# Centred sums of squares on ScalarE in the norm statistics, without VectorE's variance steps and two shift columns

## The chip, the core and the metric

One core of one Trainium2 chip runs one fused transformer block. The metric is the device time of one execution in microseconds. Before the change the median of three runs is 200.81 us (200.79 to 201.29).

The engines are named as in the profile: PE (TensorE matmuls), PEld (its weight loads), DVE (VectorE), ACT (ScalarE), POOL (GpSimd) and SP (SyncE, which issues DMAs). Each engine works through its own queue in order.

## What is computed

The reference, cut to its core (S = 2048 rows, D = 512, 32 heads of 16, F = 1792, all bf16):

```python
def _layernorm(x, eps=1e-05):
    m = mean(x); v = var(x)
    return (x - m) / sqrt(v + eps)

sa, ca, ga, sb, cb, gb = (silu(c) @ w_mod) split in six
h = _layernorm(x) * (1 + ca) + sa
x = x + ga * A(h)          # qkv; attention over 8 keys, 2 apart, looking back; output projection
h = _layernorm(x) * (1 + cb) + sb
x = x + gb * B(h)          # B: layernorm again, then an MLP over the rows (2048 -> 1792 -> 2048)
```

So each row tile passes three layernorms: of the input (called 1 in the names), of the sum after attention (2), and inside B (3).

## The kernel before

The 2048 rows are 16 tiles of 128 rows, one row per partition. They are worked in five chunks of 2, 4, 4, 4 and 2 tiles (SIZES). For each chunk: norm 1, a transposition, q, k and v (names qkv, their copies out of PSUM ev), products of q and shifted k on DVE (qk), their sums over a head on PE (red), softmax (max, sub, exp, esum, rcp, smB), products of the weights with shifted v on DVE (pv), their sums on PE (pvacc), the output projection (wo) with the residual (x1), norm 2 with its scale and shift (aff), and norm 3. The MLP's first matmul sums over all 2048 rows, so its parts (mlp1) start as soon as tiles leave norm 3; mlp2 and the output follow.

**What sets the order.** Every piece of work is put into a graph as a named operation with the engines that could run it (lines 43 to 84). The string ORDER (lines 192 to 251) lists all names in the order in which they are issued; a letter behind the colon picks the engine (`ln3s1:a` on ACT, `n1_2:d` on DVE, `n2_1:p` on POOL). `schedule` (line 86) walks the string, hands out PSUM and SBUF slots, and each engine's queue is the string filtered by engine. "fill" entries are matmuls without use, which keep PE at work. All instructions are recorded by one helper at line 143, so the profile has L143 for nearly every line, and groups are told apart by tile names.

**The norms.** The names that matter are these; the number at the end is the row tile, or the first tile of the group.

- `ln1s`, `ln2s`, `ln3s` (`ln_stats`, line 387): the statistics of one tile. On DVE one bn_stats. On ACT two passes over the tile: an Identity scaled by 1/D whose accumulator gives the mean (tile mv, column 0), and a Square scaled by D to the power -0.5 whose accumulator gives the mean of squares (tile st6).
- `ln1v`, `ln3v` (line 405): a small DVE operation. After bn_stats it is bn_aggr; after the ACT passes it computes mean of squares minus square of the mean into mv, column 1.
- `x1` and `ln2q` (lines 862 to 878): for norm 2 of tiles 0 to 13. The copy of the projection out of PSUM accumulates the row sum (tile sums, column 0), and a Square pass on ACT (`ln2q`) accumulates D times the sum of squares (column 1).
- `ln2m` (lines 887 to 896): two small DVE operations for each group of tiles, the square of the sum and its difference from column 1.
- `rstd` (`ln_rstd`, line 407): two small ACT operations, Ln of the variance plus eps, and Exp of -0.5 times that.
- `nb` (line 418): a small DVE operation, minus mean times rstd.
- `n1`, `n2`, `h3` (`ln_norm`, line 422): the normalised tile, x times rstd plus nb, on ACT, DVE or POOL.

In the profile the tiles of these are mv, st, lv, rs, nb, sums, junk (the unused full-size output of the ACT passes), xx (the rows), and h (h2, h3 and their rings).

The places that the prediction uses stand like this in ORDER:

- Around `max1` (the softmax of chunk 1, with statistics of chunk 3 among it): `... ln1s14:a ... ln1v14 nb1_3 ... mrows1 ... ln1v15 vd0_1 max1 sub1:q ...`
- Around the copy of the last columns of k for chunk 3 (`halo_k3`, on ACT, which overwrites a part of k and so waits for DVE's `qk2_2`): `x1_1:a ln2q1:a x1_0:a xt10 ln2q0:a qk2_1 ... qk2_2 a2_1_0:s halo_k3:a ln2m0 vd1_2 ... pv1_2 rstd1_4 ... nb1_4 ... rstd2_0`
- Around `max3`: `... ln2m2 pv2_0 pvacc2_0 vd3_0 ev4_20:a ln3s0:a ln3v0 ev4_12:a rstd2_2 ev4_22:a ln3v1 ... ln2m4 rstd2_4 nb2_2 n2_2:a max3 sub3:q`
- Around `qk4_1`: `... pv3_3 red4_0 ln2m6 ... qk4_1 ... rstd2_6 ... nb2_6 ... qk4_2 ... qk4_3`

Of the kernel before, what the change touches and what calls it, by code (L numbers as in the profile page):

```python
# [198 lines left out]
qvb_cp0:a ev0_00:a ln1s12:a ev0_02:d qkv1_13 ld_wqkv2 qkv0_20 ln1v13 qk0_3 qk0_2 ev1_13:a qk0_0 qvb1 ln1v12 qkv0_22:q
ld_wrow0 red0_0 ev1_00:a qkv1_03:q ev1_10:a qk0_1 red0_1 red0_2 red0_3 mask qvb_cp1:a ev0_20:a ev0_22:a wsc1_2:p  # L200
halo_v1:a qk1_0 ev1_03:a wsc1_3:a qkv1_11:q ld_wmod2 wsc2_3:a modrow0 ld_b1 mrows0:a ev1_11:a ld_wrow2 qkv1_02:q max0
wsc0_2:p ld_wo0 n1_7:p sub0:q rstd1_3 qkv1_01:q ld_wo2 exp0 qkv1_12:q wsc1_1:p esum0:q qk1_3 red1_0 ev1_01:a qk1_1
ev1_02:a biascols:q n1_6:p ld_wrow1 rcp0 smB0 ev1_12:a ld_x_4_14 ln1s14:a qkv1_22:q qk1_2 a2_0_2:a xt6 ld_wrow3 modrow1
red1_1 a2_0_1:a n1_9:p wsc2_0:d ln1s15:a ln1v14 nb1_3 n1_11:a qkv1_23:q mrows1 qkv1_21:q ev1_21:a red1_2 red1_3 xt8
ev1_23:a fill:1:q n1_10:p qkv1_20:q ev1_20:a ev1_22:a qkv2_13:q qkv2_10:q wsc0_1:p vd0_2 ev2_13:a ln1v15 vd0_1 max1
sub1:q qkv2_00:q exp1 a2_0_0:s a2_0_3:s pv0_1 vd0_0 pv0_0 st_row0 pv0_2 qkv2_03:q esum1:q ld_wo3 pvacc0_0 vd0_3
halo_v2:p biascols_cp:a pvacc0_1 pv0_3 pvacc0_2 pvacc0_3 ev2_10:a ev2_00:a qk2_0 n1_13:a n1_12:a ld_row0 woq_s rcp1
smB1 oev0_2:a qkv2_11:q qkv2_02:q ev2_03:a qk2_3 qkv2_01:q red2_0 oev0_0:a wo0:q wsc2_1:a wsc2_2:a qkv2_12:q ev2_11:a
ev2_01:a ev2_02:a ev2_12:a wo1:q qkv2_21:q a2_1_1:a qkv2_22:q x1_1:a ln2q1:a x1_0:a xt10 ln2q0:a qk2_1 qkv2_23:q xt12
qk2_2 a2_1_0:s halo_k3:a ln2m0 vd1_2 a2_1_2:s qkv3_12:q a2_1_3:s pv1_2 rstd1_4 red2_1 nb1_4 vd1_0 st_row1 red2_2 red2_3  # L210
rstd2_0 ev2_22:a nb2_0 ev2_21:a qkv3_13:q ev3_13:a max2 vd1_3 pv1_0 n1_14:a vd1_1 pvacc1_2 n1_15:a qkv2_20:q ev2_20:a
sub2:q qkv3_22:q ev3_12:a pv1_1 qkv3_10:q exp2 ev2_23:a halo_v3:a qkv3_20:q n2_0:a oev1_2:a ev3_10:a esum2:q rcp2
qkv3_00:q ev3_22:a qkv3_02:q ev3_00:a pv1_3 ev3_02:a pvacc1_0 ev3_20:a qkv3_01:q ev3_01:a qkv3_11:q xt14 ld_row1 n2_1:p
vd2_3 pvacc1_1 smB2 aff0 qk3_0 vd2_1 fill:1:q vd2_0 oev1_0:a oev1_1:a pvacc1_3 ev3_11:a qk3_1 qkv3_23:q oev1_3:a
a2_2_2:s ln3s1:a qkv3_03:q wo4:q a2_2_1:s qk3_2 a2_2_0:s ev3_03:a ev3_23:a x1_4:a ln2q4:a wo2:q x1_2:a a2_2_3:s red3_0
wo3:q x1_3:a ln2q3:a qkv3_21:q ev3_21:a wo5:q red3_1 pv2_3 x1_5:a vd2_2 qk3_3 qkv4_20:q red3_2 qkv4_22:q red3_3
qkv4_12:q fill:18:q ln2q5:a ld_w1_0_512 ln2q2:a ln2m2 pv2_0 pvacc2_0 vd3_0 ev4_20:a ln3s0:a ln3v0 ev4_12:a rstd2_2
ev4_22:a ln3v1 qkv4_02:q oev2_0:a ln2m4 rstd2_4 nb2_2 n2_2:a max3 sub3:q exp3 pvacc2_3 oev2_3:a qkv4_10:q pv2_2 vd3_2
esum3:q nb2_4 pv2_1 vd3_1 n2_3:p ld_w1_0_0 n2_5:a rcp3 smB3 pvacc2_2 fill:14:q a2_3_0:s a2_3_1:s a2_3_3:s n2_4:a
qkv4_00:q oev2_2:a rstd3_0 aff2 pvacc2_1 oev2_1:a wo6:q wo9:q wo7:q aff4 nb3_0 ln3s2:d ev4_02:a ln3s3:a ln3v3 h3_1:p  # L220
wo8:q a2_3_2:s ev4_00:a ln3v2 ld_w2_0 ln3s4:d rstd3_2 nb3_2 x1_9:a ln3s5:a h3_0:p mlp1_0_6_0:q x1_7:a ln3v4 x1_8:a
h3_3:d mlp1_0_1_0:q h3_2:d mlp1_0_6_2:q mlp1_0_1_2:q pv3_1 mlp1_0_5_0:q ln3v5 ev4_10:a ld_w1_0_896 x1_6:a mlp1_0_3_0:q
mlp1_0_3_2:q ln2q7:a pvacc3_1 rstd3_4 mlp1_0_5_2:q oev3_1:a mlp1_0_2_0:q pv3_0 mlp1_0_2_2:q nb3_4 h3_4:a mlp1_0_0_0:q
mlp1_0_0_2:q h3_5:a mlp1_0_0_4:q qk4_0 ln2q8:a ln2q6:a park0_0:a ln2q9:a mlp1_0_6_4:q mlp1_0_2_4:q mlp1_0_1_4:q
park0_1:a pv3_2 mlp1_0_5_4:q vd3_3 pvacc3_0 oev3_0:a mlp1_0_3_4:q ld_w2_1 park0_2:a pv3_3 red4_0 ln2m6 pvacc3_2
oev3_2:a mlp1_0_4_0:q qk4_1 pvacc3_3 ld_w1_0_1152 mlp1_0_4_2:q mlp1_0_4_4:q rstd2_6 oev3_3:a wo12:q halo_v4:p vd4_2
vd4_3 nb2_6 n2_9:a qk4_2 n2_7:d qk4_3 wo10:qn red4_1 ld_w1_0_1408 n2_6:a vd4_1 n2_8:a aff6 red4_2 red4_3 max4 park0_3:a
ln3s8:d ln3s6:d x1_12:a ln3v8 wo11 vd4_0 ln3s9:d mlp1_0_7_0 ld_w2_3 park0_4:a ln3v6 mlp1_0_7_2 park0_5:a ln3v9 x1_11:a
ln2q12:a mlp1_0_8_0 mlp1_0_8_2 park0_6:a wo13:n ln3s7:a ln3v7 sub4 mlp1_0_10_0 mlp1_0_9_0 x1_13:d exp4 rstd3_6 nb3_6
esum4 mlp1_0_8_4 ln2q13:a ln2m12 mlp1_0_10_2 mlp1_0_10_4 mlp1_0_9_2 rcp4 mlp1_0_7_4 h3_8:d rstd2_12 mlp1_0_12_0  # L230
mlp1_0_12_2 mlp1_0_12_4 smB4 a2_4_1:a a2_4_0:s mlp1_0_9_4 a2_4_2:s h3_9:d a2_4_3:a h3_7:d nb2_12 h3_6:p mlp1_0_7_6
ln2q11:a park0_7:a x1_10:d mlp1_0_8_6 ld_w1_0_1664 ln2q10:a park0_8:a n2_13:p mlp1_0_9_6 park0_9:a n2_12:d aff12 ln2m10
rstd2_10 mlp1_0_10_6 park0_10:a ln3s13:a pv4_2 nb2_10 ld_w1_1_0 pv4_1 mlp1_0_11_0 mlp1_0_11_2 mlp1_0_11_4 mlp1_0_12_6
# [3 lines left out]
ln3v13 park0_12:a mlp1_1_3_6 park0_13:a mlp1_1_6_6 inj1_1:n mlp1_1_1_6 n2_15:p mlp1_1_4_6 inj1_0:n mlp1_1_0_6 nb3_10
h3_10:a mlp1_1_4_10 mlp1_1_3_10 ln3s14:d ld_w2_4 mlp1_1_0_10 ln3v14 ln3v12 rstd3_12 h3_11:a mlp1_1_6_10 inj1_5:n
mlp1_1_5_6 mlp1_1_5_10 rstd3_14 mlp1_1_1_10 aff15 nb3_12 ln3s15:d ln3v15 h3_12:p nb3_14 park1_0:+ h3_13:p rstd3_15
nb3_15 inj1_2:n mlp1_1_2_6 ld_w1_1_896 h3_14:p h3_15:a ld_w1_2_0 park1_1:+ mlp1_1_2_10 park1_2:+ mlp1_1_7_10 park1_3:+  # L240
park1_4:+ park1_5:+ mlp1_1_8_10 mlp1_1_10_10 park1_6:+ padd1_7 padd1_10 gelu10 padd1_8 mlp1_1_9_10 padd1_9 gelu9
mlp1_2_4_11 mlp1_2_4_14 mlp1_2_1_11 mlp1_2_1_14 padd2_1 padd2_4 gelu7 mlp1_2_0_11 mlp1_2_0_14 padd2_0 gelu0 mlp1_2_2_11
gelu4 gelu8 mlp1_2_2_14 ld_w1_1_1408 mlp1_2_3_11 mlp1_2_3_14 padd2_3 gelu3 ld_w1_2_640 mlp1_2_6_11 padd2_6 gelu6
padd2_2 gelu2 mlp1_2_5_11 mlp1_1_11_10 padd1_11 mlp1_2_5_14 padd2_5 gelu1 gelu11 mlp1_1_12_10 ld_w2_5 ld_w2_7
mlp1_1_13_10 gelu5 mlp2_0_0 padd1_12 gelu12 mlp2_0_0b ld_w2_2 ld_w2_9 ld_w2_13 ld_w2_11 padd1_13 gelu13 mlp2_0_0c
mlp2_6_0 mlp2_4_0 gsc fin0_0 st_out0_0 fin4_0 st_out4_0 mlp2_8_0 fin8_0 mlp2_3_0 fin3_0 mlp2_2_0 fin2_0 st_out2_0
# [830 lines left out]
```

## Time and profile before

| what | value |
|---|---|
| median of 3 runs | 200.81 us |
| the profiled execution | 201.21 us |
| its span, first to last instruction | 199.3 us |
| granted clock of PE | 1.0 throughout |
| DMA | 36.02 MB, 181 GB/s in the mean |

How to read the lines quoted below. Times are in us from the start of the span unless a column says ns. A line of the windows view is a stretch, its length, the busy time and number of instructions of each engine in the order PE, PEld, DVE, ACT, POOL, then the clock, the DMA share and GB/s. A line of the chain of waits is a start, a length and the work that the end of the program depended on there. A line of the groups is engine, operation, tiles out<-in, shapes and count, then total busy us and mean ns of one, then idle time before. A line of the timeline is start, length, engine, operation, tiles, shape and count, with the engine's idle time before it and what ended that in brackets. Neighbouring DVE and ACT instructions overlap by about 0.1 us in the records, so what one instruction costs its engine is the distance from its start to the next one's start.

### The profile page before, as it was taken

How to read it: one execution, taken by the hardware profiler on the slowest of the kernel's cores; microseconds unless marked ns; L12 is line 12 of the kernel's file. 1: busy time of each engine (PE TensorE's matmuls, PEld its weight loads, DVE VectorE, ACT ScalarE, POOL GpSimd, SP SyncE). 2: the span in 40 equal slices, each digit the busy share in tenths (PEclk: the TensorE clock that was granted, in tenths of full speed). 3: DMA queues.
4: the chain of work that ended last, by engine and by line, in shares of the span. 5: the costliest groups of instructions: out<-in, count | busy, mean ns of one | idle time of the engine just before them, and what ended most of it. 6: DMA issues, size and time to landing. Idle time of an engine off the chain costs nothing.

```text
span 199.3 us, 5635 instructions
## 1 busy us (share of the span) xinstructions
...
## 2 busy tenths in 40 slices
...
GB/s 170 319 362 329 210 272 102 161 56 224 263 192 302 241 195 143 162 144 302 49 325 242 45 199 174 161 208 223 337 239 311 82 19 53 26 56 52 172 53 53
DMA packets 53893, 36.02 MB, mean 181 GB/s; under 512 B 24428, under 2 KB 50668, under 8 KB 53868
## 3 DMA queue, kind: packets, MB, share of 16 engines
...
q10 hardware_dynamic: 1640, 0.46, 1.0%
q8 instruction: 18, 0.29, 0.7%
q14 instruction: 7, 0.06, 0.1%
...
## 4 chain that ended last, share of the span: by engine, by line
PE 64%; DVE 21%; issue 5%; ACT 4%; DMA 3%; SPq 1%; DVEq 0%; ACTq 0%
PE psS L143 62%; DVE big L143 15%; DMA xx<-in_A_x_dram 3%; PE psL L143 2%; DVE h L143 2%; DVE lsb L143 1%; SPq L143 1%; DVE mv L143 1%; ACT h L143 1%; ACT v_sb L143 1%; ACT k_f L143 1%; DVE st L143 1%; DVE m L143 1%; ACT hT L143 1%; ACT junk L143 0%
## 5 line engine op out<-in xcount | busy, mean ns | idle before, releaser
L143 PEld LDWEIGHTS <-wst 128*128 128x128 bf16 (+1 forms) x584 | 35.6, 101 | 33.5 <-issue 2.8
L143 PE MATMUL psS<-h,wst 128*32 128x512 bf16 (+1 forms) x362 | 50.7, 379 | 0.4 <-ACT h L143 0.3
L143 DVE TENSOR_TENSOR big<-a2sb,vD 128x4096 bf16<-128x4096 bf16 (+1 forms) x20 | 36.5, 1858 | 0.2
L143 DVE TENSOR_TENSOR big<-q_sb,k_f 128x4096 bf16<-128x4096 bf16 (+1 forms) x20 | 36.6, 1856 | 0.1
L143 DVE SCALAR_TENSOR_TENSOR h<-psS,bcol,rows_bc 128x512 f32<-128x512 f32 (+2 forms) x17 | 12.1, 710 | 22.1 <-PE psS L143 22.0
L143 PE MATMUL psS<-hT,w_qkv 128*32 128x512 bf16 (+1 forms) x576 | 29.5, 344 | 0.0
L143 PEld LDWEIGHTS <-w_qkv 128*32 128x32 bf16 (+1 forms) x618 | 22.0, 107 | 13.8 <-issue 0.2
L143 PE MATMUL psS<-gT,big 128*128 128x512 bf16 x112 | 25.0, 379 | 0.0
L143 PEld LDWEIGHTS <-big 128*128 128x128 bf16 x144 | 12.0, 97 | 14.4 <-DMA big<-in_w_mod_dram 1.2
L143 ACT ACTIVATE junk<-xx 128x512 bf16<-128x512 bf16 x26 | 16.3, 628 | 4.1 <-issue 1.5
L143 PE MATMUL psS<-woq,o_sb 128*32 128x512 bf16 (+1 forms) x208 | 16.7, 379 | 0.5 <-ACT o_sb L143 0.5
L143 ACT ACTIVATE gT<-psS,bcol 128x512 bf16<-128x512 f32 x14 | 9.0, 685 | 8.1 <-DVE psS L143 8.0
L143 POOL TENSOR_SCALAR h<-xx,rs,nb 128x512 bf16<-128x512 bf16 x9 | 7.0, 781 | 73.2 <-DVE nb L143 34.4
L143 DVE TENSOR_TENSOR psS<-psS,gT 128x512 f32<-128x512 f32 x14 | 9.3, 695 | 5.0 <-PE psS L143 5.0
L143 PEld LDWEIGHTS <-group 128*32 128x32 bf16 x288 | 7.9, 96 | 9.0 <-issue 3.3
L143 PE MATMUL psS<-hT,wst 128*32 128x512 bf16 (+2 forms) x136 | 12.1, 356 | 0.2 <-ACT hT L143 0.2
L143 ACT ACTIVATE h<-xx,nb,rs 128x512 bf16<-128x512 bf16 x15 | 11.6, 811 | 0.3 <-DVE nb L143 0.2
L143 DVE BATCH_NORM_STATS2 st<-xx 128x6 f32<-128x512 bf16 x12 | 8.0, 683 | 4.4 <-DMA xx<-in_A_x_dram 4.4
L143 DVE TENSOR_TENSOR h<-h,xx 128x512 bf16<-128x512 f32 (+2 forms) x17 | 11.1, 652 | 0.6
L143 DVE TENSOR_TENSOR h<-h,rows_bc 128x1024 bf16<-128x1024 bf16 (+2 forms) x16 | 10.9, 688 | 0.4
L143 PE MATMUL psL<-big,group 128*32 128x512 bf16 x128 | 9.7, 380 | 1.6 <-DVE big L143 1.3
L143 ACT ACTIVATE v_sb<-psS,qvb 128x512 bf16<-128x512 f32 (+1 forms) x20 | 11.0, 595 | 0.0
...
## 6 DMA issues: line engine op xcount, KB each, us to landing
...
```

The source lines that it names most:

```text
L143: r = fn(*a, **k)
```

## The change

On ACT, the second pass of the statistics squares the distance from the mean (scale -1 and the mean as a bias column) in place of the value. This is done for all 14 `ln2q` passes and, in norms 1 and 3, for three groups listed in CENT: tiles 14 and 15 of norm 1, tiles 0 and 1 of norm 3, tiles 12 and 13 of norm 3. The accumulator then holds the sum of squared distances itself, so the variance operations of those tiles (`ln1v14`, `ln1v15`, `ln3v0`, `ln3v1`, `ln3v12`, `ln3v13`) and all six `ln2m` pairs go from DVE, and `rstd` of those groups reads what ACT has written. In the groups 1_1 and 3_2 (NONB) the column nb goes as well: the tiles that are normalised on DVE there take (x - mean) * rstd. That is 20 small DVE instructions fewer, and one more column operand on 20 ACT passes. ORDER loses the tokens of the removed operations; nothing else in it moves, and the queues of PE, POOL and SP hold the same instructions in the same order.

```diff
+    CENT=((0, 14), (2, 0), (2, 12)),
+    NONB=("1_1", "3_2",),
...
-    def ln_stats(l, st, src, reads, name):
+    def ln_stats(l, g0, st, src, reads, name):
         st6, mv = ln_t["st6", l], ln_t["mv", l]
+        if (l, g0) in CENT:
+            def fc():
+                nc.scalar.activation(junk[:], src, ACT.Identity, scale=1.0 / D, accum_out=mv[:, st, 0:1])
+                nc.scalar.activation(junk[:], src, ACT.Square, scale=-1.0, bias=mv[:, st, 0:1], accum_out=mv[:, st, 1:2])
+            add("act", 1.26, fc, ...)
+            return
...
+        if (l, g0) in CENT:
+            vscale, vreads = 1.0 / D, [("stt", l, st) for st in range(g0, g0 + n)]
...
+        if name in NONB:
+            return
...
+        if f"{l + 1}_{g0 if l else T0.index(g0)}" in NONB:
+            m_ = ln_t["mv", l][:, st, 0:1]
+            G.add("dve", 0.42, lambda: nc.vector.tensor_scalar(dst, src, m_, r_, op0=ALU.subtract, op1=ALU.mult), ...)
+            return
...
-                nc.scalar.activation(junk[:], xx[:, st, :], ACT.Square, scale=D ** 0.5, accum_out=sums[:, st, 1:2])
+            add("act", 0.73, lambda st=st: nc.scalar.activation(junk[:], xx[:, st, :], ACT.Square, scale=-float(D),
+                                                                bias=sums[:, st, 0:1], accum_out=sums[:, st, 1:2]),
...
-                    nc.vector.tensor_tensor(mv[:, gs, 0], sums[:, gs, 0], sums[:, gs, 0], op=ALU.mult)
-                    nc.vector.tensor_tensor(mv[:, gs, 1], mv[:, gs, 0], sums[:, gs, 1], op=ALU.subtract)
-                add("dve", 0.2 if gn == 1 else 0.4, f, ..., name=f"ln2m{g0}")
-                ln_rstd(1, g0, gn, f"2_{g0}", [("mv", 1, st) for st in gt], -1.0 / D ** 2)
+                ln_rstd(1, g0, gn, f"2_{g0}", sums[:, g0:g0 + gn, 1], 1.0 / D ** 3,
+                        [(k, st) for k in ("sum0", "sum1") for st in gt])
```

More of the change, by code (lines that the diff above doesn't have):

```diff
@@ L199 @@
[L199 to L233, printed above, removed]
+ln1s5:d ln1v4 ln1v5 ln1v3 ln1v2 rstd1_1 ld_x_2_6 a1col n1_2 n1_5 ln1s8:a wsc0_3:p n1_4 hT0_1:a hT0_3:a n1_3 hT0_0:a
@@ new lines @@
+ev1_03:a wsc1_3:a qkv1_11:q ld_wmod2 wsc2_3:a modrow0 ld_b1 mrows0:a ev1_11:a ld_wrow2 qkv1_02:q max0 wsc0_2:p ld_wo0
+n1_7:p sub0:q rstd1_3 qkv1_01:q ld_wo2 exp0 qkv1_12:q wsc1_1:p esum0:q qk1_3 red1_0 ev1_01:a qk1_1 ev1_02:a biascols:q
+n1_6:p ld_wrow1 rcp0 smB0 ev1_12:a ld_x_4_14 ln1s14 qkv1_22:q qk1_2 a2_0_2:a xt6 ld_wrow3 modrow1 red1_1 a2_0_1:a
+n1_9:p wsc2_0:d ln1s15 nb1_3 n1_11:a qkv1_23:q mrows1 qkv1_21:q ev1_21:a red1_2 red1_3 xt8 ev1_23:a fill:1:q n1_10:p
+qkv1_20:q ev1_20:a ev1_22:a qkv2_13:q qkv2_10:q wsc0_1:p vd0_2 ev2_13:a vd0_1 max1 sub1:q qkv2_00:q exp1 a2_0_0:s
@@ new lines @@
+a2_0_3:s pv0_1 vd0_0 pv0_0 st_row0 pv0_2 qkv2_03:q esum1:q ld_wo3 pvacc0_0 vd0_3 halo_v2:p biascols_cp:a pvacc0_1 pv0_3
+pvacc0_2 pvacc0_3 ev2_10:a ev2_00:a qk2_0 n1_13:a n1_12:a ld_row0 woq_s rcp1 smB1 oev0_2:a qkv2_11:q qkv2_02:q ev2_03:a
+qk2_3 qkv2_01:q red2_0 oev0_0:a wo0:q wsc2_1:a wsc2_2:a qkv2_12:q ev2_11:a ev2_01:a ev2_02:a ev2_12:a wo1:q qkv2_21:q
+a2_1_1:a qkv2_22:q x1_1:a ln2q1 x1_0:a xt10 ln2q0 qk2_1 qkv2_23:q xt12 qk2_2 a2_1_0:s halo_k3:a vd1_2 a2_1_2:s
+qkv3_12:q a2_1_3:s pv1_2 rstd1_4 red2_1 nb1_4 vd1_0 st_row1 red2_2 red2_3 rstd2_0 ev2_22:a nb2_0 ev2_21:a qkv3_13:q
@@ new lines @@
+ev3_13:a max2 vd1_3 pv1_0 n1_14:a vd1_1 pvacc1_2 n1_15:a qkv2_20:q ev2_20:a sub2:q qkv3_22:q ev3_12:a pv1_1 qkv3_10:q
+exp2 ev2_23:a halo_v3:a qkv3_20:q n2_0:a oev1_2:a ev3_10:a esum2:q rcp2 qkv3_00:q ev3_22:a qkv3_02:q ev3_00:a pv1_3
+ev3_02:a pvacc1_0 ev3_20:a qkv3_01:q ev3_01:a qkv3_11:q xt14 ld_row1 n2_1:p vd2_3 pvacc1_1 smB2 aff0 qk3_0 vd2_1
+fill:1:q vd2_0 oev1_0:a oev1_1:a pvacc1_3 ev3_11:a qk3_1 qkv3_23:q oev1_3:a a2_2_2:s ln3s1 qkv3_03:q wo4:q a2_2_1:s
+qk3_2 a2_2_0:s ev3_03:a ev3_23:a x1_4:a ln2q4 wo2:q x1_2:a a2_2_3:s red3_0 wo3:q x1_3:a ln2q3 qkv3_21:q ev3_21:a wo5:q
@@ new lines @@
+red3_1 pv2_3 x1_5:a vd2_2 qk3_3 qkv4_20:q red3_2 qkv4_22:q red3_3 qkv4_12:q fill:18:q ln2q5 ld_w1_0_512 ln2q2 pv2_0
+pvacc2_0 vd3_0 ev4_20:a ln3s0 ev4_12:a rstd2_2 ev4_22:a qkv4_02:q oev2_0:a rstd2_4 nb2_2 n2_2:a max3 sub3:q exp3
+pvacc2_3 oev2_3:a qkv4_10:q pv2_2 vd3_2 esum3:q nb2_4 pv2_1 vd3_1 n2_3:p ld_w1_0_0 n2_5:a rcp3 smB3 pvacc2_2 fill:14:q
+a2_3_0:s a2_3_1:s a2_3_3:s n2_4:a qkv4_00:q oev2_2:a rstd3_0 aff2 pvacc2_1 oev2_1:a wo6:q wo9:q wo7:q aff4 nb3_0
+ln3s2:d ev4_02:a ln3s3:a ln3v3 h3_1:p wo8:q a2_3_2:s ev4_00:a ln3v2 ld_w2_0 ln3s4:d rstd3_2 x1_9:a ln3s5:a h3_0:p
@@ new lines @@
+mlp1_0_6_0:q x1_7:a ln3v4 x1_8:a h3_3 mlp1_0_1_0:q h3_2 mlp1_0_6_2:q mlp1_0_1_2:q pv3_1 mlp1_0_5_0:q ln3v5 ev4_10:a
+ld_w1_0_896 x1_6:a mlp1_0_3_0:q mlp1_0_3_2:q ln2q7 pvacc3_1 rstd3_4 mlp1_0_5_2:q oev3_1:a mlp1_0_2_0:q pv3_0
+mlp1_0_2_2:q nb3_4 h3_4:a mlp1_0_0_0:q mlp1_0_0_2:q h3_5:a mlp1_0_0_4:q qk4_0 ln2q8 ln2q6 park0_0:a ln2q9 mlp1_0_6_4:q
+mlp1_0_2_4:q mlp1_0_1_4:q park0_1:a pv3_2 mlp1_0_5_4:q vd3_3 pvacc3_0 oev3_0:a mlp1_0_3_4:q ld_w2_1 park0_2:a pv3_3
+red4_0 pvacc3_2 oev3_2:a mlp1_0_4_0:q qk4_1 pvacc3_3 ld_w1_0_1152 mlp1_0_4_2:q mlp1_0_4_4:q rstd2_6 oev3_3:a wo12:q
@@ new lines @@
+halo_v4:p vd4_2 vd4_3 nb2_6 n2_9:a qk4_2 n2_7:d qk4_3 wo10:qn red4_1 ld_w1_0_1408 n2_6:a vd4_1 n2_8:a aff6 red4_2
+red4_3 max4 park0_3:a ln3s8:d ln3s6:d x1_12:a ln3v8 wo11 vd4_0 ln3s9:d mlp1_0_7_0 ld_w2_3 park0_4:a ln3v6 mlp1_0_7_2
+park0_5:a ln3v9 x1_11:a ln2q12 mlp1_0_8_0 mlp1_0_8_2 park0_6:a wo13:n ln3s7:a ln3v7 sub4 mlp1_0_10_0 mlp1_0_9_0 x1_13:d
+exp4 rstd3_6 nb3_6 esum4 mlp1_0_8_4 ln2q13 mlp1_0_10_2 mlp1_0_10_4 mlp1_0_9_2 rcp4 mlp1_0_7_4 h3_8:d rstd2_12
+mlp1_0_12_0 mlp1_0_12_2 mlp1_0_12_4 smB4 a2_4_1:a a2_4_0:s mlp1_0_9_4 a2_4_2:s h3_9:d a2_4_3:a h3_7:d nb2_12 h3_6:p
@@ L237 @@
[L237 to L246, printed above, removed]
@@ L405, in ln_stats, with ln_rstd @@
         add("dve", 0.15, fv, reads=[("stt", l, st)], writes=[("mv", l, st)], name=name[:3] + "v" + name[4:])
-    def ln_rstd(l, g0, n, name, vreads=None, vscale=1.0):
+    def ln_rstd(l, g0, n, name, var=None, vscale=1.0, vreads=None):
         mv, lv, rs, nb = (ln_t[k, l] for k in ("mv", "lv", "rs", "nb"))
         sl = slice(g0, g0 + n)
-        var = mv[:, sl, 1]
+        if (l, g0) in CENT:
+            vscale, vreads = 1.0 / D, [("stt", l, st) for st in range(g0, g0 + n)]
         def fa():
-            nc.scalar.activation(lv[:, sl, 0], var, ACT.Ln, scale=vscale, bias=epscol[:, 0:1])
+            nc.scalar.activation(lv[:, sl, 0], mv[:, sl, 1] if var is None else var, ACT.Ln, scale=vscale, bias=epscol[:, 0:1])
             nc.scalar.activation(rs[:, sl, 0], lv[:, sl, 0], ACT.Exp, scale=-0.5)
```

62 lines of the change are left out of this document (33 added, 29 removed).

## The prediction

> **What bounds the kernel now.** I read three views in this order: busy time by stretches, the chain of waits, and the timeline of single engines. First the stretches, in the middle of the attention and in the MLP.
>
> ```profile
> 60.00:67.00 7.00, 7.00 (x140) 4.51 (x132) 6.96 (x6) 6.97 (x15) 0.00 (x0) 1.00 0.83 282
> 97.00:104.00 7.00, 6.71 (x115) 3.15 (x108) 6.90 (x9) 6.78 (x16) 0.00 (x0) 1.00 0.69 213
> 130.00:145.00 15.00, 15.00 (x71) 6.86 (x70) 10.39 (x17) 7.91 (x12) 0.66 (x1) 1.00 0.92 264
> ```
>
> The reader is to see that in the attention (60 to 67, 97 to 104) PE, DVE and ACT are all full at once: time taken from DVE and given to ACT is not taken from an idle engine and given to an idle one. From 130 on only PE is full. The end of the chain of waits says where that begins:
>
> ```profile
> 103.09 0.40 PE psL L143 x4
> ...
> 107.48 88.81 PE psS L143 x478
> ```
>
> From 103.09 the end hangs on PE alone, 88.81 us of it in one piece. What comes after 103.09 keeps its length, so the change is worth what it moves that point. Who held PE there stands in PE's timeline:
>
> ```profile
> 102.20 0.61 PE L143 MATMUL psL<-big,group 128*32 128x512 bf16 x8
> 103.09 0.40 PE L143 MATMUL psL<-big,group 128*32 128x512 bf16 x4 [0.29 <-DVE big L143]
> ```
>
> It waited 0.29 us for DVE's last product of chunk 4 (`qk4_3`). The question is how much earlier DVE reaches that product, and whether PE is there by then.
>
> **The price on ACT.** Twenty Square passes get a column as bias. No pass with accumulator and bias column is in the trace, so I bound it by pairs of rows with and without columns:
>
> ```profile
> L143 ACT ACTIVATE junk<-xx 128x512 bf16<-128x512 bf16 x26 | 16.3, 628 | 4.1 <-issue 1.5 <-DVE xx L143 1.4 <-DMA xx<-in_A_x_dram 0.6
> L143 ACT ACTIVATE h<-xx,nb,rs 128x512 bf16<-128x512 bf16 x15 | 11.6, 811 | 0.3 <-DVE nb L143 0.2
> ```
>
> ```profile
> L143 ACT ACTIVATE gT<-psS 128x512 bf16<-128x512 f32 x14 | 8.0, 585 | 0.1
> L143 ACT ACTIVATE q_sb<-psS,qvb 128x512 bf16<-128x512 f32 x12 | 7.9, 689 | 0.0
> ```
>
> Two columns make 811 of 628 ns, 0.09 us each; one column makes 689 of 585, 0.10. I take 0.09 per pass (the pair that reads the same memory), with 0 as the low end, if the fetch hides in the wait that these passes have anyway for the accumulator before them, and 0.18 as the high end, the whole distance of the first pair. Sub-then-multiply in the two NONB groups I take at the price of multiply-then-add, since both have two columns; I see no reason for a gain or a loss, and at 0.1 us either way for all six it would stay inside the range.
>
> **The saving on DVE, step by step.** The price of a removed instruction is the distance to the next start. The first two are `ln1v14` and `ln1v15`, just ahead of `max1`:
>
> ```profile
> 32.81 1.05 PE L143 MATMUL psL<-big,group 128*32 128x512 bf16 x16
> ```
>
> ```profile
> 33.93 0.23 DVE L143 SCALAR_TENSOR_TENSOR mv<-mv,st 128x1 f32<-128x1 f32 x1
> 34.08 1.21 DVE L143 TENSOR_REDUCE m<-psL 128x128 bf16<-128x1024 f32 x1
> ```
>
> Without them DVE is free before 33.9, but the maximum needs PE's sums, which end at 32.81 + 1.05 = 33.86; with some 0.05 for the release it starts at 33.91, so DVE gains 0.17. Next the pair `ln2m0`:
>
> ```profile
> 50.34 0.15 DVE L143 TENSOR_TENSOR mv<-sums 128x2 f32<-128x2 f32 x1
> ...
> 50.89 2.29 DVE L143 TENSOR_TENSOR big<-a2sb,vD 128x4096 bf16<-128x4096 bf16 x1
> ```
>
> It is worth 0.55, if the product's loads have landed by then; they were issued microseconds before, and I let it stand. DVE is now 0.72 ahead. The pair `ln2m2`, then `ln3v0`, `ln3v1` and the pair `ln2m4`:
>
> ```profile
> 73.92 0.15 DVE L143 TENSOR_TENSOR mv<-sums 128x2 f32<-128x2 f32 x1
> ...
> 74.28 2.29 DVE L143 TENSOR_TENSOR big<-a2sb,vD 128x4096 bf16<-128x4096 bf16 x1
> 76.49 0.34 DVE L143 SCALAR_TENSOR_TENSOR mv<-mv,st 128x1 f32<-128x1 f32 x2
> ...
> 77.01 0.15 DVE L143 SCALAR_TENSOR_TENSOR nb<-sums,rs 128x2 f32<-128x2 f32 x1
> ```
>
> They are 0.36 and 0.52, and DVE could stand at `nb2_2` (the row at 77.01) 0.72 + 0.36 + 0.52 = 1.60 earlier, at 75.41. Here the change meets its own price, for `nb2_2` needs `rstd2_2` from ACT, and `max3` with the rest of chunk 3 is queued behind it on DVE.
>
> **What ACT does meanwhile.** Two rows of its timeline, 25 us apart:
>
> ```profile
> 50.45 0.26 ACT L143 ACTIVATE k_f<-k_f 128x64 bf16<-128x64 bf16 x1 [1.16 <-DVE big L143]
> ```
>
> ```profile
> 75.06 0.19 ACT L143 ACTIVATION_READ_ACCUMULATOR junk<-h 128x1 f32 x1
> 75.59 0.60 ACT L143 ACTIVATE k_f<-psS 128x512 bf16<-128x512 f32 x1 [0.34 <-PE psS L143]
> 76.08 0.29 ACT L143 ACTIVATE lv<-mv,epscol 128x2 f32<-128x2 f32 x1
> 76.40 0.20 ACT L143 ACTIVATE rs<-lv 128x2 f32<-128x2 f32 x1
> ```
>
> At 50.45 ACT had waited 1.16 us for DVE (`halo_k3`). That wait covers the four longer passes before it (`ln1s14`, `ln1s15`, `ln2q1`, `ln2q0`: 0.36), and because DVE is 0.17 ahead, so is ACT from here. Until 75.25 it has next to no idle time and gets six longer passes (`ln3s1`, `ln2q4`, `q3`, `q5`, `q2`, `ln3s0`): 6 x 0.09 = 0.54. Before, it was free for the copy at 75.59 about 0.43 early (the read ends at 75.25, and a successor may overlap by 0.09) and waited 0.34 of that for PE, which itself had been held by DVE and now comes earlier. So the copy starts at 75.16 - 0.17 + 0.54 = 75.53, and the Exp ends at 76.60 - 0.06 = 76.54. `nb2_2` starts at about 76.57, not at 75.41: DVE has a **new stall of 1.16 us** and keeps 0.44 of the 1.60.
>
> Two more places. In group 3_2 the column `nb3_2` is gone, and the two tiles wait for the Exp alone:
>
> ```profile
> 87.17 0.30 ACT L143 ACTIVATE lv<-mv,epscol 128x2 f32<-128x2 f32 x1 [0.17 <-DVE mv L143]
> ```
>
> ```profile
> 87.74 0.25 DVE L143 SCALAR_TENSOR_TENSOR nb<-mv,rs 128x2 f32<-128x2 f32 x1
> 87.91 0.17 DVE L143 BATCH_NORM_AGGREGATE mv<-st 128x2 f32<-128x6 f32 x1
> ```
>
> ACT's Ln waited for DVE and moves with it, by 0.44; DVE gains 0.17 more and is 0.61 ahead. Then the pair `ln2m6`, and behind `qk4_1` again a column that waits for ACT:
>
> ```profile
> 92.80 0.58 ACT L143 ACTIVATE o_sb<-psS 128x512 bf16<-128x512 f32 x1
> 93.39 0.81 ACT L143 ACTIVATE h<-h,nb,rs 128x512 bf16<-128x512 bf16 x1
> ```
>
> ```profile
> 99.61 0.21 ACT L143 ACTIVATE rs<-lv 128x4 f32<-128x4 f32 x1
> ```
>
> ```profile
> 98.82 0.15 DVE L143 TENSOR_TENSOR mv<-sums 128x4 f32<-128x4 f32 x1
> ...
> 99.16 1.22 DVE L143 TENSOR_TENSOR big<-q_sb,k_f 128x2048 bf16<-128x2048 bf16 x1
> 100.29 0.15 DVE L143 SCALAR_TENSOR_TENSOR nb<-sums,rs 128x4 f32<-128x4 f32 x1
> ```
>
> ACT carries 0.44 from 87.17, loses 0.36 to `ln2q7`, `q8`, `q6` and `q9`, and wins the 0.1 for which the tile at 93.39 stood after its forerunner had let go. Its Exp ends at 99.82 - 0.18 = 99.64, so `nb2_6` starts at 99.67, 0.62 earlier; what `ln2m6` saves (0.34) goes into the wait. `qk4_3` and PE's matmul at 103.09 move by **0.6 us**. PE is ready: it had 0.29 to spare there, and its last hold ahead of that was on ACT, for the tile at 93.39, which comes 0.45 earlier (0.44 - 0.09 for `ln2q7` + 0.1):
>
> ```profile
> 94.97 1.26 PE L143 MATMUL psS<-h,wst 128*32 128x512 bf16 x20 [0.26 <-ACT h L143]
> ```
>
> No step is moved past another: the queues of PE, POOL and SP are unchanged. `nb1_1` stands in the loading stage; I count it at nothing, at most at the 0.17 of `nb3_2`. What goes after 107 (`ln2m12`, `ln2m10`, `ln3v12`, `ln3v13`) lies beside PE's unbroken piece.
>
> A rule that speaks against this reading: the Trainium skill ("Trainium Kernel Development and Optimization", Performance Expectations) holds matmul busy time for a bad measure of how near PE is to its limit and wants the busy share of the weight loads. By that PE from 130 to 145 would be at 6.86 of 15.00, not at its limit, which is the fourth rival below. The trace does not agree here, since PE waits for nobody in that stretch while DVE has 4.6 us to spare.
>
> **The sum.** The profiled execution took 201.21 us with a span of 199.3, so 1.9 lie around it, untouched. Minus 0.6 it would be 200.6. It stands 0.4 above the median of the runs, so I forecast 200.81 - 0.6 = **200.2 us** for the median.
>
> **Rivals.**
> 1. ACT has room after all (a pass with bias costs near 0, or ACT keeps up otherwise), and DVE's saving passes whole: 0.17 + 0.55 + 0.36 + 0.52 + 0.17 + 0.34 = 2.1, **198.7**. For it: DVE has hardly a gap. Against it: ACT at 6.97 of 7.00.
> 2. Slower: a pass with bias costs 0.18. Then the copy at 75.59 starts 0.48 late (75.16 - 0.17 + 1.08), the Exp ahead of `nb2_2` ends at 77.08 and DVE is 0.1 late there. ACT makes up the wait of 0.17 at 87.17 and the 0.1 at 93.39, loses 0.72 to four passes, and its Exp ends 0.9 late, at 100.75; `nb2_6` and the matmul at 103.09 come 0.5 late: **201.3**. It decides from about 0.13 per pass, where by the same steps `nb2_6` stands where it stood. For it: ACT is the engine that the change loads, in its fullest stretch, and any further lateness of its copies holds PE's slots. Against it: both pairs say 0.09 to 0.10.
> 3. PE does not follow: its copies out of PSUM come from ACT, and the gain at 103.09 ends as PE's own lateness; 0 to 0.2 remain, **200.7**. For it: PE was held by ACT at 94.97. Against it: the 0.29 us of room.
> 4. PE after 107 is not the bound. Then two more pairs (0.34 each by the rows at 98.82 and 99.16) and two single steps (0.15 each by 33.93) count, 1.0 more: **199.2**. Against it: 88.81 us in one piece.
>
> That the operations do not go at all is excluded: DVE's built queue is 20 instructions shorter.
>
> **How the numbers follow.** Forecast 0.46, rivals 0.17, 0.17, 0.16 and 0.04. About 0.3% (0.6 us) is what a measurement can tell from no change. The forecast sits on that border, so half of it counts as faster: 0.23 + 0.17 + 0.04 = 0.44 faster; 0.23 + 0.16 + 0.05 of rival 2 = 0.44 the same; the rest of rival 2, where more than 0.18 is lost in the coupled stretch, 0.12 slower. The range 198.9 to 201.3 leaves out half of rival 1 and over half of rival 2, about 0.2.
>
> **What would show it.** Right: the 20 passes at about 0.72 us; a stall of about 1 us on DVE ahead of the column near 76.5 put down to ACT's rs; another near 99; the last run of PE starting 0.6 us earlier. Wrong: no stall on DVE at either place (rival 1), ACT's passes at 0.8 us (rival 2), or a wait of PE for ACT's copies between 95 and 103 in place of that for DVE (rival 3).

## The result, and the profile after

| | before | after |
|---|---|---|
| median of 7 runs | 200.79 us (200.44 to 201.33) | 199.72 us (199.59 to 200.12) |
| the profiled execution | 201.21 us | 199.64 us |
| its span | 199.3 us | 197.9 us |

The ratio is 0.9948 with a 95% interval of 0.9932 to 0.9965: 1.07 us faster, where 0.6 was forecast.

**How much of the profiles' difference is the change.** The two spans differ by 1.4 us, but part of that lies in the loading stage, ahead of nearly all that was changed. A fixed early event shows it: PE's matmul of the mask, in PE's timeline of the kernel before, of the changed kernel, and of one more execution of the kernel before (the run "before again").

```profile
23.77 0.22 PE L143 MATMUL psL<-mask,ident 32*32 32x128 bf16 x1
```

```profile
23.25 0.22 PE L143 MATMUL psL<-mask,ident 32*32 32x128 bf16 x1
```

```profile
23.31 0.22 PE L143 MATMUL psL<-mask,ident 32*32 32x128 bf16 x1
```

The end of the work is DVE's last addition of the output, in DVE's timeline of the same three profiles:

```profile
196.31 0.29 DVE L143 TENSOR_TENSOR h<-psS,fpre 128x128 bf16<-128x128 f32 x1
```

```profile
194.89 0.29 DVE L143 TENSOR_TENSOR h<-psS,fpre 128x128 bf16<-128x128 f32 x1
```

```profile
195.87 0.29 DVE L143 TENSOR_TENSOR h<-psS,fpre 128x128 bf16<-128x128 f32 x1
```

The same kernel started 0.46 us apart in two executions, yet from mask to end it took 172.54 and 172.56 us. The changed kernel took 171.64. So I compare profiles by this distance: the change is worth **0.90 us** of it, and the other 0.52 of the span is the start of these two executions. Times below that are called "net" have 0.52 taken off.

**The stretches** (the windows view of the changed kernel, columns as before):

```profile
60.00:67.00 7.00, 7.00 (x140) 4.57 (x136) 6.96 (x6) 6.97 (x16) 0.00 (x0) 1.00 0.86 275
97.00:104.00 7.00, 6.95 (x101) 3.47 (x98) 6.80 (x9) 6.97 (x17) 0.00 (x0) 1.00 0.90 256
130.00:145.00 15.00, 14.89 (x70) 6.78 (x70) 10.73 (x17) 7.74 (x13) 0.00 (x0) 1.00 1.02 291
```

From 97 to 104 PE went from 6.71 to 6.95 and ACT from 6.78 to 6.97, while DVE, which was to be relieved, is the one with most room (6.80). The changed kernel is some 1.4 us further on in its work there, so these sums only hint; single rows show why. First DVE's timeline of the changed kernel:

```profile
75.84 0.16 DVE L143 SCALAR_TENSOR_TENSOR nb<-sums,rs 128x2 f32<-128x2 f32 x1 [0.88 <-ACT rs L143]
75.92 1.22 DVE L143 TENSOR_REDUCE m<-psL 128x128 bf16<-128x1024 f32 x1
...
98.86 0.17 DVE L143 SCALAR_TENSOR_TENSOR nb<-sums,rs 128x4 f32<-128x4 f32 x1 [0.17 <-ACT rs L143]
```

Then the groups on ACT, where the price stands:

```profile
L143 ACT ACTIVATE junk<-xx,sums 128x512 bf16<-128x512 bf16 x14 | 10.1, 722 | 1.6 <-DVE xx L143 1.4
L143 ACT ACTIVATE junk<-h 128x512 bf16<-128x512 bf16 x12 | 7.6, 635 | 0.3
```

DVE, for which the profile before lists no wait between 60 and 100 us, now waits twice for the Exp of ACT. A pass with a bias column takes 722 ns against 628 to 635 without. Last, the chain of waits of the changed kernel from the middle on:

```profile
75.81 0.73 ACT v_sb L143 x2
77.35 0.80 ACT h L143
...
81.52 0.68 DVE lsb L143
82.84 1.30 DVE h L143 x2
...
92.30 1.42 ACT h L143 x2
93.76 3.09 PE psS L143 x52
97.06 4.32 PE psS L143 x76
101.38 0.69 PE psL L143 x12
102.44 3.40 PE psS L143 x15
```

The end now hangs on PE from 93.76 on instead of 103.09, and ahead of that on ACT, with one stretch of DVE between 81.5 and 86. PE's red products of chunk 4, which had waited 0.29 us for DVE, run on without a wait.

### The profile page after: what moved, and what is told of

It is laid out like the page before. It is cut to its first block, busy times and chain, and to the rows that moved or that the text cites. A ratio compares the mean times of both kernels' runs of the same rounds, so it can differ in the third digit from the quotient of the medians.

```text
span 197.9 us, 5606 instructions
## 1 busy us (share of the span) xinstructions
PE 187.8 (95%) x2348; PEld 101.9 (51%) x2358; DVE 157.5 (80%) x222; ACT 127.8 (65%) x305; POOL 18.5 (9%) x45
## 4 chain that ended last, share of the span: by engine, by line
PE 64%; ACT 19%; DVE 5%; DMA 4%; SPq 3%; issue 3%; ACTq 0%; DVEq 0%
PE psS L143 63%; ACT junk L143 4%; DMA vD<-v_sb 3%; SPq L143 3%; ACT xx L143 2%; ACT v_sb L143 2%; ACT h L143 2%; DVE big L143 2%; PE psL L143 2%; ACT q_sb L143 2%; ACT k_f L143 2%; DVE h L143 1%; ACT o_sb L143 1%; DMA c_t<-in_c_dram 1%; ACT lsb L143 1%
## 5 line engine op out<-in xcount | busy, mean ns | idle before, releaser
L143 ACT ACTIVATE junk<-xx,sums 128x512 bf16<-128x512 bf16 x14 | 10.1, 722 | 1.6 <-DVE xx L143 1.4
L143 PEld LDWEIGHTS <-ident 128*32 128x32 bf16 (+2 forms) x242 | 7.1, 99 | 7.4 <-issue 2.8
```

The lines of the kernel that those rows point to most:

```text
L143: r = fn(*a, **k)
```

## The experiments

Two theories went in. **A:** in the changed kernel ACT sets the pace between 50 and 94 us; what DVE saves comes back as its stalls, and the price of the longer passes counts only since DVE has become the earlier engine. **B:** DVE is still the bound, each removed operation is worth its length. Each run below is compared with runs of the kernel before on the same chip. "Net" is the change of the distance from the mask to the last addition in the profile, against 172.54.

| kernel | ratio, 95% interval | mask | last addition | net |
|---|---|---|---|---|
| the change | 0.9948 (0.9932 to 0.9965) | 23.25 | 194.89 | -0.90 |
| column nb1_1 back | 0.9947 (0.9917 to 0.9976) | 23.24 | 194.85 | -0.93 |
| price alone | 0.9986 (0.9964 to 1.0008) | 23.81 | 196.38 | +0.03 |
| saving alone | 0.9885 (0.9851 to 0.9919) | 23.13 | 194.03 | -1.64 |
| max3 first | 0.9900 (0.9866 to 0.9933) | 23.27 | 194.43 | -1.38 |
| ln2m0 back | 0.9958 (0.9940 to 0.9976) | 25.07 | 196.91 | -0.70 |
| four back | 0.9945 (0.9929 to 0.9961) | 23.98 | 195.58 | -0.94 |
| six only | 0.9944 (0.9924 to 0.9963) | 23.27 | 195.00 | -0.81 |
| max3 first, n2_5 on DVE | 0.9922 (0.9898 to 0.9946) | 23.16 | 194.58 | -1.12 |
| max3 first, no price | 0.9901 (0.9877 to 0.9925) | 23.17 | 194.22 | -1.49 |
| six only, max3 first | 0.9964 (0.9950 to 0.9978) | 23.33 | 195.57 | -0.30 |
| max3 and qk4_2 first | 0.9945 (0.9924 to 0.9966) | 23.45 | 195.33 | -0.66 |

The ratios lie 0.1 to 0.3% lower than the net distances say, for every kernel, the one with the price alone too; what in the start or the end makes up that part was not settled. The order among the kernels is nearly the same either way. Many of the ratios' intervals overlap, so a difference of 0.1 to 0.3 net between two kernels rests on one profile of each and on the rows that show where it arises. For the kernel before, the distance repeated to 0.02 us, but two profiles stand behind the kernel that they vary by more than that at 70 us already, ahead of the first thing that differs: "max3 first, n2_5 on DVE" by 0.06 and "six only, max3 first" by 0.13.

**Does the early start come from nb1_1?** The column goes back; then the kernel before is run once more.

```diff
-    NONB=("1_1", "3_2",),
+    NONB=("3_2",),
```

> The changed kernel with the column nb1_1 put back on VectorE (its three tiles of norm 1 take x times rstd plus nb again); the rest of the change stays. Why: the profile of the changed kernel is already 0.52 us early at 23 us, in the loading stage, where only nb1_1 has gone. Theory A (nb1_1 is hidden by the loading, the early start is a difference between two executions): 199.7 us, between 199.5 and 199.9, as the changed kernel with 199.72. Theory B (nb1_1 is worth the 0.5 us): 200.2 us, so half of the whole gain or all of it would be this one column.

> The kernel before once more, for a second profile. In the profiles so far the kernels with the change stand 0.50 to 0.65 us ahead of the kernel before from 12 us on, where nothing of the change has run but one column, and putting that column back did not take the lead away. Theory A (the loading stage differs by half a microsecond from one execution to the next): this profile can begin either way; PE's matmul of the mask near 23 us stands at 23.77 or at 23.25, and with 23.25 the span is 198.7 to 198.9 in place of 199.3. Theory B (the kernel before always begins late): 23.77 again and a span of 199.3. One more profile can show A but not prove B.

Column back: 199.82 us, mask at 23.24. Before again: mask at 23.31, as shown above. Theory A holds in both: the early start belongs to the execution, and nb1_1 is worth nothing. (The group has four tiles on DVE, `n1_2` to `n1_5`, and not the three of the text above.)

**The price without the saving, and the saving without the price.**

```diff
 # price alone: the kernel before, with a column of zeros (the 14 ln2q passes shown; the 6 in ln_stats likewise)
-nc.scalar.activation(junk[:], xx[:, st, :], ACT.Square, scale=D ** 0.5, accum_out=sums[:, st, 1:2])
+nc.scalar.activation(junk[:], xx[:, st, :], ACT.Square, scale=D ** 0.5, bias=zcol[:, 0:1], accum_out=sums[:, st, 1:2])
 # saving alone: the changed kernel, without the columns (so its variance lacks the square of the mean); likewise in ln_stats
-nc.scalar.activation(junk[:], xx[:, st, :], ACT.Square, scale=-float(D), bias=sums[:, st, 0:1], accum_out=...)
+nc.scalar.activation(junk[:], xx[:, st, :], ACT.Square, scale=-float(D), accum_out=...)
```

> The kernel before with a column of zeros as bias of the same 20 Square passes; all of VectorE's operations stay, so this is the price without the saving. Theory A (ScalarE had room as long as VectorE was the later one: 1.16 us at the copy for chunk 3, 0.34 at 75.59, 0.47 between its Exp and nb2_6): 0 to 0.3 us over the kernel before, 200.8 to 201.1. Theory B (ScalarE set the pace already): ten of the passes lie between 50 and 97 us, 10 x 0.09 = 0.9 us over, 201.7.

> The changed kernel with the bias columns taken out again: the 20 passes square the value itself, and the square of the mean is left out of the variance of these tiles; VectorE's operations stay away. This is the saving without the price. Theory A (in the changed kernel ScalarE is the bound between 50 and 94 us, and VectorE's stalls of 0.88 us ahead of nb2_2 and 0.17 ahead of nb2_6 are its lateness): the ten passes between 50 and 97 us give 0.09 us each, the stalls shrink to near 0, and the time falls by 0.7 to 0.9, to 198.8 to 199.0. Theory B (VectorE and PE are the bound, the stall only stands in place of a later wait): 199.5 to 199.7, as the changed kernel.

The same twenty longer passes cost +0.03 net (0.9986) where DVE is the later engine, and 1.64 - 0.90 = 0.74 net (0.9885 against 0.9948) where it has been relieved. The saving alone still leaves a stall on DVE, half as long:

```profile
75.26 0.16 DVE L143 SCALAR_TENSOR_TENSOR nb<-sums,rs 128x2 f32<-128x2 f32 x1 [0.44 <-ACT rs L143]
```

Theory A holds for both. A price cannot be read off by adding it to the old kernel alone: there its cover was the very lateness of DVE that the change takes away.

**Which of the removed operations count?** Small operations are put back at their old places, on a tile that nobody reads; or only a part of the change is made.

```diff
 # ln2m0 back
-... qk2_2 a2_1_0:s halo_k3:a vd1_2 ...
+... qk2_2 a2_1_0:s halo_k3:a ln2m0 vd1_2 ...
 # four back
-... ln2q2 pv2_0 ... ln3s0 ev4_12:a rstd2_2 ev4_22:a ... oev2_0:a rstd2_4 nb2_2 ...
+... ln2q2 ln2m2 pv2_0 ... ln3s0 ln3v0 ev4_12:a rstd2_2 ev4_22:a ln3v1 ... oev2_0:a ln2m4 rstd2_4 nb2_2 ...
 # six only
-    CENT=((0, 14), (2, 0), (2, 12)),        # and all ln2q
+    CENT=((0, 14),),                        # and ln2q0, ln2q1
```

> The changed kernel with the two small operations of ln2m0 put back at their old place on VectorE, on a tile that nobody reads. Theory A (VectorE's 0.55 us at 50 us also set ScalarE free, which had waited for nb1_4 and for PE at 53 to 55; that is why ScalarE came to 74.8 with 0.26 to 0.40 us of lead in place of the 0.06 to 0.17 forecast): ScalarE falls back by 0.2 to 0.3 us near 55 and keeps that to the end, 199.9 to 200.0 us. Theory B (as the prediction has it, this lead ends in VectorE's stall ahead of nb2_2): no loss, 199.7 us, the stall is 0.3 instead of 0.88.

> The changed kernel with the small operations of ln2m2, ln3v0, ln3v1 and ln2m4 put back at their old places on VectorE, on a tile that nobody reads: six of the twenty, 0.36 + 0.52 = 0.88 us by their rows in the kernel before, all of them ahead of nb2_2, where VectorE waits 0.88 us for ScalarE's Exp. Theory A (they were worth nothing, for the stall took what they saved): 199.7 to 199.85 us, and the stall of 0.88 is gone. Theory B (the stall is not the end of it; VectorE's lead is worth its length further on): 200.3 us or more.

> Only a part of the change: the distance from the mean is squared for tiles 14 and 15 of norm 1 and tiles 0 and 1 of norm 2 (4 of the 20 passes, those ahead of ScalarE's wait of 1 us at the copy of k for chunk 3), and the columns nb1_1 and nb3_2 are gone. The other sixteen passes and thirteen small operations are as in the kernel before. Theory A (the other operations save what is lost again in the stalls, and their sixteen longer passes buy nothing): VectorE is 0.17 + 0.55 = 0.72 us ahead at nb2_2 and finds its Exp done, 0.17 more comes from nb3_2, so 0.9 us under the kernel before and as fast as the changed kernel, 199.6 to 199.9. Theory B (every removed operation counts by its length): 0.9 of 2.1 us of saving, so 0.45 of the gain that was measured, 200.3 us.

Four back costs nothing (-0.94 against -0.90): the six operations stand where the stall was, and `nb2_2` behind them waits for nobody, as DVE's timeline of that run shows:

```profile
75.97 0.34 DVE L143 SCALAR_TENSOR_TENSOR dum<-mv 128x1 f32<-128x1 f32 x2
76.23 0.15 DVE L143 TENSOR_TENSOR dum<-sums 128x2 f32<-128x2 f32 x1
76.42 0.16 DVE L143 TENSOR_TENSOR dum<-dum,sums 128x2 f32<-128x2 f32 x1
76.53 0.16 DVE L143 SCALAR_TENSOR_TENSOR nb<-sums,rs 128x2 f32<-128x2 f32 x1
```

ln2m0 back costs 0.20 of its 0.55, so not all of it ended in the stall, as the prediction had it (theory A, its place is shown below). The run that makes only a part of the change leaves out six operations, not seven, and keeps fourteen: DVE has 242 instructions before, 222 in the changed kernel and 236 in this run, which is called "six only" here. It keeps 0.81 of the 0.90, with 4 of the 20 longer passes and 6 of the 20 operations removed. The other fourteen operations, with their sixteen passes, buy some 0.1 us at most, and the ratios (0.9944 against 0.9948) show no difference.

**Filling the stall.** `max3` needs nothing from ACT, so it can go ahead of `nb2_2`; then the same for `qk4_2` and `nb2_6`; and the first on the kernel with six removed, which has no stall.

```diff
-... oev2_0:a rstd2_4 nb2_2 n2_2:a max3 sub3:q exp3 ...
+... oev2_0:a rstd2_4 max3 sub3:q nb2_2 n2_2:a exp3 ...
 # max3 and qk4_2 first, also
-... vd4_3 nb2_6 n2_9:a qk4_2 n2_7:d ...
+... vd4_3 qk4_2 nb2_6 n2_9:a n2_7:d ...
```

> The changed kernel with max3 and sub3 issued ahead of nb2_2 and n2_2: VectorE takes the maximum of chunk 3 in the 0.88 us in which it waited for ScalarE's Exp. No work changes. Theory A (ScalarE is the bound there): VectorE's lead ends at its next wait for ScalarE, near nb2_6; what passes is ScalarE's own wait of 0.17 us for VectorE at 86.0, so 199.5 us, 0.0 to 0.3 under the changed kernel. Theory B (VectorE is the bound and the new stall costs its whole length): 198.8 us, 0.9 under it.

> The run with seven operations removed and four longer passes (199.86 us), with max3 and sub3 ahead of nb2_2 and n2_2 as well. There VectorE has no stall at nb2_2. Theory A (the order is worth the stall that it fills): 0 to 0.1 us of gain, or a small loss because nb2_2 and with it n2_2 on ScalarE come up to 1.1 us later than its Exp; 199.8 to 200.3. Theory B (issuing max3 early is good by itself, since sub3, exp3 and the rest of chunk 3 hang on it): about the 0.5 to 0.6 us that it gave on the changed kernel, 199.3.

> The run with max3 first, with qk4_2 issued ahead of nb2_6 and n2_9 too, so that VectorE fills its second stall (0.16 us) as well. nb2_6 then comes about 1.0 us later and ScalarE's three tiles of norm 2 behind it stand. Theory A (ScalarE has no time to lose there: its copies out of PSUM and its tiles of norm 2 are queued behind n2_9): the 0.16 is lost again or more, 199.1 to 199.9. Theory B (what counts is only when VectorE reaches qk4_3): 0.15 under the run with max3 first, 198.95.

max3 first: 199.09 us, 0.48 net under the changed kernel and the fastest of the kernels that leave nothing out; neither theory had its size. With six only, where there is no stall, the same order gains nothing and the end comes 0.51 later net, so theory B is out. But the loss does not come the way theory A gave, by a late `nb2_2` and `n2_2`. Of it 0.13 is there at 70 us, ahead of the swap. The rest arises in one place, DVE's softmax scaling `smB3`, which takes 1.10 us here and 0.69 in six only, beside a tile of POOL, as DVE's and POOL's timelines of this run show:

```profile
81.66 1.10 DVE L143 TENSOR_TENSOR lsb<-lsb,rb 128x1024 bf16<-128x1024 bf16 x1
```

```profile
77.43 4.79 POOL L143 TENSOR_SCALAR h<-xx,rs,nb 128x512 bf16<-128x512 bf16 x1 [24.32 <-issue]
```

So the order gives something only where it fills a stall, and it has a price of its own, which is taken up below. With `qk4_2` first as well, 0.72 is lost, and all three engines show one wait each, on DVE, ACT and PE in turn:

```profile
101.96 1.23 DVE L143 TENSOR_TENSOR h<-h,rows_bc 128x2048 bf16<-128x2048 bf16 x1 [0.64 <-ACT h L143]
```

```profile
99.70 0.81 ACT L143 ACTIVATE h<-xx,nb,rs 128x512 bf16<-128x512 bf16 x1 [0.63 <-DVE nb L143]
```

```profile
102.46 0.59 PE L143 MATMUL psS<-woq,o_sb 128*128 128x512 bf16 x2 [0.66 <-ACT gT L143]
```

The late column holds ACT's tiles, ACT's copies behind them come late, and PE waits for their slot. So the end does not hang on DVE's products alone at that point.

**Why max3 first gained 0.48.** In the changed kernel DVE's softmax scaling (`smB3`, lsb at 81.52 in the chain above) stood 0.76 us after `rb` from ACT was there (in the run with max3 first the wait for it ends at 80.76). That lateness was the stall, passed on to `aff2`, to the Ln of group 3_2 and to PE. With max3 first DVE gets there 0.76 earlier, but loses 0.3 at once. Its timeline and POOL's in that run:

```profile
76.09 2.28 DVE L143 TENSOR_TENSOR big<-a2sb,vD 128x4096 bf16<-128x4096 bf16 x1
78.29 0.15 DVE L143 SCALAR_TENSOR_TENSOR nb<-sums,rs 128x2 f32<-128x2 f32 x1
78.37 2.28 DVE L143 TENSOR_TENSOR big<-a2sb,vD 128x4096 bf16<-128x4096 bf16 x1
80.76 0.98 DVE L143 TENSOR_TENSOR lsb<-lsb,rb 128x1024 bf16<-128x1024 bf16 x1
81.67 1.41 DVE L143 TENSOR_TENSOR h<-h,rows_bc 128x1024 bf16<-128x1024 bf16 x2
```

```profile
76.33 4.87 POOL L143 TENSOR_SCALAR h<-xx,rs,nb 128x512 bf16<-128x512 bf16 x1 [23.37 <-PE psS L143]
```

POOL's tile `n2_3` now begins beside the products instead of beside `max3` and lasts 4.87 us instead of 0.77, and `smB3`, which overlaps its end, takes 0.98 instead of 0.68. So 0.76 - 0.3 = 0.46 arrives at `aff2`. That POOL's tile makes `smB3` longer is read from rows of three runs (0.98, 1.10 and, with `qk4_2` first as well, 0.95 us) and not from a run that moves the tile. It fits that with n2_5 on DVE, where `smB3` starts after POOL's tile has ended (81.22 against 81.15), it takes 0.67 again.

**Is ACT the only bound with max3 first?** One tile goes from ACT to DVE; or the price is taken out there.

```diff
 # max3 first, and
-... n2_3:p ld_w1_0_0 n2_5:a rcp3 smB3 ...
+... n2_3:p ld_w1_0_0 n2_5:d rcp3 smB3 ...
```

> The kernel of the run with max3 first (199.09 us), with one normalised tile of norm 2 (n2_5) moved from ScalarE to VectorE: it takes 0.70 us from ScalarE and gives VectorE some 0.32 (the same operation on VectorE stands at that distance in the profiles). Theory A (with max3 first both engines are full from 60 to 101 us; VectorE's only waits for ScalarE there are 0.11 us at smB3 and 0.16 at nb2_6): VectorE has no room for 0.32, the time stays within 0.15 of 199.1. Theory B (ScalarE alone is the bound, as in the changed kernel): 0.4 to 0.7 under it, 198.4 to 198.7.

> The run with max3 first, with the bias columns taken out as in the run of the saving alone (the square of the mean is left out of the variance of these tiles). Theory A (both engines full): without the price ScalarE comes 0.9 us earlier, VectorE can use only its two waits, 0.11 + 0.16 = 0.27, so 198.5 to 198.8, no better than the saving alone with the old order (198.78) by more than 0.2. Theory B (ScalarE alone is the bound): the whole price of 0.7 to 0.9 again, 198.2 to 198.4.

The tile on DVE makes it slower by 0.26 net (-1.12 against -1.38), of which 0.06 is there before the tile; that is a little more than theory A allowed. The tile took 0.70 us of DVE (80.52 to 81.22), not 0.32, beside POOL's tile, which ends at 81.15 in this run (76.28 + 4.87). Taking the price out gives 0.11 net and nothing in the ratio (0.9901 against 0.9900), less than either theory. A third engine held it at `aff2`, which starts 0.17 later than with max3 first, measured from the mask; DVE's and POOL's timelines in that run:

```profile
81.74 1.42 DVE L143 TENSOR_TENSOR h<-h,rows_bc 128x1024 bf16<-128x1024 bf16 x2 [0.60 <-POOL h L143]
```

```profile
76.23 5.48 POOL L143 TENSOR_SCALAR h<-xx,rs,nb 128x512 bf16<-128x512 bf16 x1 [23.36 <-PE psS L143]
```

So with max3 first ACT is not the only bound any more; POOL's tile `n2_3`, next to DVE's products, comes next. Giving that tile to another engine was not tried.

## Why the prediction was right, and where it was short

- **The price per pass.** Forecast 0.09 us; 722 against 628 to 635 ns is 0.09. The Trainium skill ("ScalarE: Activation LUTs", What ACT_TABLE_LOAD costs) gives about 93 ns for a column operand; the trace agrees, also for passes with an accumulator.
- **max1 held by PE, 0.17.** From 34.08 to 33.38 is 0.70, 0.18 net. Right.
- **ln2m0, 0.55 on DVE.** `pv1_2` went from 50.89 to 49.65: 1.24, 0.72 net, as summed up there. Right.
- **ACT 0.17 ahead from the copy at 50.45 on, with next to no idle time up to 75.25.** This is the step that failed, in size. ACT did wait between 50 and 55, in gaps so short that the timeline prints no bracket for them. The rows behind the copy, before (where the copy stands at 50.45, shown above), after, and with ln2m0 back:

```profile
53.29 1.52 ACT L143 ACTIVATE h<-xx,nb,rs 128x512 bf16<-128x512 bf16 x2
54.77 0.69 ACT L143 ACTIVATE v_sb<-psS,qvb 128x512 bf16<-128x512 f32 x1
```

```profile
49.76 0.26 ACT L143 ACTIVATE k_f<-k_f 128x64 bf16<-128x64 bf16 x1 [0.98 <-DVE big L143]
...
52.44 1.52 ACT L143 ACTIVATE h<-xx,nb,rs 128x512 bf16<-128x512 bf16 x2
53.85 0.69 ACT L143 ACTIVATE v_sb<-psS,qvb 128x512 bf16<-128x512 f32 x1
```

```profile
51.58 0.26 ACT L143 ACTIVATE k_f<-k_f 128x64 bf16<-128x64 bf16 x1 [0.98 <-DVE big L143]
...
54.42 1.52 ACT L143 ACTIVATE h<-xx,nb,rs 128x512 bf16<-128x512 bf16 x2
55.90 0.69 ACT L143 ACTIVATE v_sb<-psS,qvb 128x512 bf16<-128x512 f32 x1
```

  From the copy to the v_sb row ACT took 4.32 us before, 4.09 after, and 4.32 again with ln2m0 back. So DVE's 0.55 at 50 us gave ACT 0.23. The tile at 53.29 had stood for DVE's column `nb1_4`, whose row ends at 53.25 (53.10 + 0.15), and the v_sb row for PE, whose matmuls end at 54.72 (53.68 + 1.04). PE had been held by DVE too, as its timelines before and after show:

```profile
53.24 0.62 PE L143 MATMUL psS<-big,group 128*32 128x512 bf16 x8 [0.86 <-ACT k_f L143]
```

```profile
51.99 0.61 PE L143 MATMUL psS<-big,group 128*32 128x512 bf16 x8 [0.29 <-DVE big L143]
```

  The profile before names ACT's copy of k, but that copy's row ends at 53.25, after PE's start, and in the changed kernel the same matmul starts 0.57 us ahead of the copy's end. What PE waited for is DVE's product, which ends at 53.18 (50.89 + 2.29). The run with ln2m0 back shows that 0.20 of the 0.23 reaches the end.
- **A new stall of 1.16 ahead of nb2_2, DVE keeps 0.44.** The profile prints 0.88, counted from the end of the product's row; counted as in the forecast, from where the next start could have been (0.08 earlier), it is 0.96. DVE kept 77.01 - 75.84 - 0.52 = 0.65. The stall was right; its length was off by the 0.2 that ACT came sooner.
- **nb3_2 worth 0.17.** The product behind it moved by 88.67 - 87.31 - 0.52 = 0.84, 0.19 more than 0.65. Right.
- **nb2_6 0.62 early, with ln2m6 lost in a wait.** It came 100.29 - 98.86 - 0.52 = 0.91 early, behind a wait of 0.17 for the Exp: right in kind, and 0.29 better, 0.2 of it from the same step at 50 us. The last 0.09 is ACT's, spread over rows between 90 and 99, and I can't put it down to one wait.
- **PE follows and the rest keeps its length.** PE's last red products have no wait any more, and the last addition moved by the 0.9 of nb2_6. So the sum should have been 0.9 in place of 0.6. The run with max3 and qk4_2 first qualifies the step: it holds only as long as ACT's copies keep up, for otherwise PE is held again at 102.46 (the third rival's mechanism, by another cause).
- **The rivals.** The first, ACT with room, is out: the price costs 0.74 net once the saving is there, and "saving alone" gave 1.64 rather than 2.1, as a stall of 0.44 was left. The second, slower at 0.18 per pass, is out by the 0.09. The fourth is out, as the end came no more than the 0.9 of `nb2_6` sooner. Six only keeps all the operations after 107: at PE's red products it stands within 0.01 us net of the changed kernel, and near 118 it is 0.08 behind, so what the rival counted at 1.0 is worth 0.1 at most.
- **The base.** The forecast took one execution's span as its base and set off the 0.4 us to the median. The start alone varies by 0.46 between two executions of the kernel before, so this 0.4 is no property of the kernel, and a sum of 0.6 can't be checked on two spans. The medians moved by 1.07, which is 0.17 more than the 0.90 that the rows account for; where that part lies is not shown.
